# Two decode layers on one core: seven of the streamed tiles are fetched by three DMAs of 112, 8 and 8 partitions instead of one DMA of 128

## The chip, the cores and the metric

The kernel runs on one core of a Trainium2 chip. The metric is the device time of one execution in microseconds; lower is better. The time before is a median of three executions, and one more execution was profiled.

## The reference, cut to what matters

Two layers of attention against a cache, each followed by a dense layer with a gelu, are run twice over the same weights and caches, for one new position of eight sequences (B = 8, D = 1024, 32 query heads, 4 key and value heads of 128, 4096 cached positions, F = 3584), all in float32:

```python
def _A_ref(x, k_cache, v_cache, wq, wo):
    q = (x @ wq).reshape(B, Sq, Hq, Dh).transpose(0, 2, 1, 3)
    k = jnp.repeat(k_cache, rep, axis=1)
    v = jnp.repeat(v_cache, rep, axis=1)
    scores = jnp.einsum("bhqd,bhkd->bhqk", q, k) * (Dh ** -0.5)
    p = _softmax(scores, axis=-1)
    o = jnp.einsum("bhqk,bhkd->bhqd", p, v)
    return o.transpose(0, 2, 1, 3).reshape(B, Sq, Hq * Dh) @ wo

def _B_ref(x, w1, b1, w2, b2):
    h = _gelu(jnp.einsum("bsd,df->bsf", x, w1) + b1)
    return jnp.einsum("bsf,fd->bsd", h, w2) + b2

x = x + _A_ref(_layernorm(x), k_cache, v_cache, wq, wo)
x = x + _B_ref(_layernorm(x), w1, b1, w2, b2)
# and the same two lines once more
```

## The kernel before, in words

Eight rows of activations meet 134 MB of cache and some 63 MB of weights in each layer, so nearly all the work is to bring tiles from HBM into SBUF and to run each through TensorE once. Every tile is 128 partitions high. A tile is either "k = 4" (four columns of the arena, 4 x 4 KB = 16 KB in each partition, 2 MB in all) or "k = 2" (8 KB in each partition, 1 MB in all).

The order of all loads is written down ahead, in the list `stream`: the weights of the query projection (`q0`), then the caches of layer 0 in the order in which `scores` and `values` use them (`caches`), then `o0`, `i0`, `p0` (output projection, first and second dense matrix), `q1`, the caches of layer 1 in reverse order of sequences without what is still held from layer 0, and `o1`, `i1`, `p1`. The function `pump` takes the next entry of the list as soon as the `Arena` has room for it and issues its load on SyncE's queue (SP), one `dma_start` for a whole tile. `release` frees a tile after its last use and calls `pump` again, so SP's instructions stand in the order of the stream, each with its wait for the tile whose place it takes. The framework counts the DMAs of a queue on eight semaphores in turn, and a DMA that uses one again waits until the DMA eight places earlier has landed.

A tile has a key. For weights it is a name and a number (`("o0", 8)` is the ninth tile of the output projection of layer 0, `(("q1", 0), 2)` the third of the first half of the query projection of layer 1). For caches it is the layer and the piece: `(0, ("k", 2, 0, 0))` is layer 0, the keys of sequence 2, heads 0 and 1, first half of the positions; `(0, ("v", 4, 3, 0))` the values of sequence 4, head 3. Sizes follow from `pairs` and from the lists in the calls of `weights`: the cache tiles of sequences 0 to 5 in layer 0 and 0 to 4 in layer 1 and the tiles of `o1` have 2 MB, those of `o0`, `i0` and `q1` 1 MB.

`scores` (L295), `values` (L349), `expand` (L213) and `project` (L266) are the matmuls that read the tiles; each waits for its whole tile. The last tiles of the stream belong to `p1`, whose matmuls feed the last addition (L275) and the store of the output (L515).

Of the kernel before, what the change touches and what calls it, by code (L numbers as in the profile page):

```python
# [14 lines left out]
P = 128  # L15
# [21 lines left out]
N_TILE = 24  # L37
N_OWN = 2
EXTRA = 7
Q_AT = (0, 48, 72, 32)  # L40
QW = 88
DMA_SCRATCH = 1024
# [41 lines left out]
def decode_layers(ctx: ExitStack, tc: tile.TileContext, x, kc, vc, wq, wo, w1, b1, w2, b2, out):  # L84


    nc = tc.nc
# [84 lines left out]
    def pump():  # L172
        while stream:
            key, k, src, limit, pack = stream[0]
            arena.limit = min(limit, arena.cap)
            slot = arena.take(k, pack=pack)
            if slot is None:
                return
            stream.pop(0)
            if callable(src):  # L180
                src(slot.ap)
            else:
                nc.sync.dma_start(out=slot.ap[:, 0:src.shape[1]], in_=src)  # L183
            held[key] = slot

    def release(slot):
        slot.free()
        pump()
# [50 lines left out]
    def query_unit(u, row):  # L239
        src = turned(row, 2 * REP)  # L240
        for e in range(2):
            c = Q_AT[2 * u + e]
            nc.vector.tensor_copy(qz_v[:, c:c + REP, :], src[:, e * REP:(e + 1) * REP])
# [35 lines left out]
    def k_at(b, r):  # L279
        return b, r % HKV, r // HKV  # L280

    def v_at(b, r):
        return b, r // NH, r % NH

    def scores(at, kt, spare=False):
# [6 lines left out]
        ps = st["ps", half]  # L292
        c = b * QW + Q_AT[j] - REP * j
        for g in range(NG):
# [180 lines left out]
    kept = {("k", *k_at(B - 1, r)) for r in range(NR)} | {("v", *v_at(B - 1, r)) for r in range(NR)}  # L475
    kept |= {("k", *k_at(B - 2, NR - 1 - e)) for e in range(EXTRA)}
    first = [("k", B - 1, j, half) for half in range(NH) for j in range(2)]
# [17 lines left out]
    weights("i1", w1, [4, 4, 4, 2], [BIG] * 2)  # L495
    weights("p1", w2, [4] * 6 + [2, 1, 1], [BIG])
    pump()
    for layer in range(2):
        st["layer"] = layer
# [69 lines left out]
```

## Time and profile before

| | |
|---|---|
| median of three executions | 886.03 us (885.03 to 888.13) |
| the profiled execution | 886.38 us, of which 884.4 us from its first to its last instruction |
| mean granted TensorE clock | 0.809 |
| TensorE busy (matmuls) | 565.8 us, 64% |
| VectorE, ScalarE busy | 180.8 us, 47.2 us |
| moved by DMA | 371.15 MB, mean 420 GB/s |
| DMA's share of the chain that ended last | 85% |

The profiled execution is 0.35 us above the median, so its rows can be read against the median as they stand. "DMA share" in a row of the profile is the mean busy share of the core's sixteen DMA engines; "us to landing" is the median time from the issue of a DMA to the landing of its last byte.

### The profile page before, as it was taken

Reading aid. Unit: us, or ns where it says so; the run is one execution under the profiler, and the core shown is the slowest. Engines: PE = TensorE matmul, PEld = TensorE weight load, DVE = VectorE, ACT = ScalarE, POOL = GpSimd, SP = SyncE. Lnnn points to the kernel's source line nnn. Section 1 sums busy time; section 2 is a strip of 40 time slices with the busy share of each in tenths; the row PEclk is TensorE's granted clock in tenths of the full one; section 3 lists DMA queues with packets and bytes.
Section 4 is the critical chain, followed back from the end, with each engine's and each line's share of the span. In section 5 each row is a group of like instructions: output and inputs, shape, how many; then the busy total and the mean of one; then the engine's idle time right before and its main releaser. Section 6 shows DMA issues by size and latency. Waiting matters only on the chain.

```text
span 884.4 us, 9323 instructions
## 1 busy us (share of the span) xinstructions
PE 565.8 (64%) x4016; PEld 179.2 (20%) x4016; DVE 180.8 (20%) x586; ACT 47.2 (5%) x75; POOL 1.6 (0%) x11
## 2 busy tenths in 40 slices
PE   4565565565675767666656679956665575756766
PEld 1111121121111112222221122211121121222322
DVE  1002122221322223200200124422122222400110
ACT  2000000000000001001000100000000000000000
POOL 0000000000000000000000000000000000000000
PEclk9787788888868676867877979988888988876786
DMA  9999999999999999999999999999999999999996
GB/s 385 423 431 429 427 426 426 429 429 427 428 426 423 422 421 421 415 416 396 422 421 417 414 422 425 423 424 430 425 429 428 426 428 429 425 428 428 425 428 289
DMA packets 34888, 371.15 MB, mean 420 GB/s; under 512 B 4000, under 2 KB 4384, under 8 KB 4640
## 3 DMA queue, kind: packets, MB, share of 16 engines
q1 hardware_dynamic: 34704, 370.44, 99.5%
q8 instruction: 31, 0.51, 0.2%
q10 hardware_dynamic: 144, 0.13, 0.0%
q14 instruction: 9, 0.07, 0.0%
HBM read 370.42 MB, written 0.13 MB: 419 GB/s over the span
## 4 chain that ended last, share of the span: by engine, by line
DMA 85%; PE 11%; DVE 2%; issue 1%; ACT 1%; SPq 0%; ACTq 0%; DVEq 0%
DMA arena<-in_A_k_cache_dram 49%; DMA arena<-in_B_w_dram 17%; DMA arena<-in_A_wo_dram 8%; DMA arena<-in_A_wq_dram 7%; DMA arena<-in_A_v_cache_dram 4%; PE o_ps L349 2%; PE sps L295 2%; PE acc L213 2%; PE y L266 2%; DVE r_o L354 1%; PE sps L328 1%; PE sps L362 0%; SPq L183 0%; ACT arena L316 0%; PE s_ps L295 0%
## 5 line engine op out<-in xcount | busy, mean ns | idle before, releaser
L295 PE MATMUL sps<-arena,qz 128*32 128x512 f32 x992 | 169.3, 765 | 164.5 <-DMA arena<-in_A_k_cache_dram 162.7
L349 PE MATMUL o_ps<-arena 128*32 128x512 f32 x1024 | 166.1, 731 | 1.4 <-DMA arena<-in_A_v_cache_dram 1.4
L266 PE MATMUL y<-arena,oT 128*32 128x256 f32 x960 | 91.6, 532 | 54.1 <-DMA arena<-in_A_wo_dram 28.9
L213 PE MATMUL acc<-arena,xnT 128*32 128x512 f32 (+3 forms) x632 | 83.1, 625 | 47.2 <-DMA arena<-in_A_wq_dram 25.9
L295 PEld LDWEIGHTS sps<-arena,qz 128*32 128x32 f32 x992 | 24.7, 122 | 225.0 <-issue 139.4
L354 DVE SCALAR_TENSOR_TENSOR r_o<-o_ps,sel_t,r_o 128x128 f32<-128x128 f32 x192 | 67.4, 351 | 6.8
L266 PEld LDWEIGHTS y<-arena,oT 128*32 128x32 f32 x960 | 35.1, 141 | 109.5 <-DMA arena<-in_A_wo_dram 40.4
L349 PEld LDWEIGHTS o_ps<-arena 128*32 128x32 f32 x1024 | 35.0, 129 | 81.6 <-issue 79.2
L363 DVE TENSOR_TENSOR oT<-sps,rl 128x8 f32<-128x8 f32 x64 | 11.0, 173 | 179.7 <-PE sps L362 179.6
L316 ACT ACTIVATE arena<-arena,bias 128x1024 f32<-128x1024 f32 x16 | 18.4, 1148 | 520.9 <-DVE nb L313 520.9
L213 PEld LDWEIGHTS acc<-arena,xnT 128*32 128x32 f32 x632 | 23.6, 128 | 97.8 <-DMA arena<-in_A_wq_dram 42.7
L362 PEld LDWEIGHTS sps<-sel_h,r_o 128*128 128x128 f32 x128 | 23.5, 230 | 82.4 <-issue 53.1
L328 PE MATMUL sps<-ident,arena 128*128 128x128 f32 x128 | 22.7, 304 | 16.8 <-ACT arena L332 11.8
L298 DVE TENSOR_SCALAR_CACHE_REDUCE arena<-sps 128x512 f32<-128x512 f32 x31 | 21.4, 692 | 56.8 <-PE sps L295 56.8
L352 DVE TENSOR_SCALAR r_o<-o_ps,sel_t 128x128 f32<-128x128 f32 x64 | 22.4, 350 | 51.1 <-PE o_ps L349 51.1
L362 PE MATMUL sps<-sel_h,r_o 128*128 128x8 f32 x128 | 29.4, 302 | 4.4 <-DVE r_o L354 3.9
L275 DVE SCALAR_TENSOR_TENSOR x_row<-y,x_row 128x256 f32<-128x256 f32 x4 | 1.7, 425 | 122.4 <-PE y L266 122.4
L226 DVE TENSOR_SCALAR row<-acc,rs 128x512 f32<-128x512 f32 (+1 forms) x8 | 5.5, 685 | 87.1 <-PE acc L213 87.1
L328 PEld LDWEIGHTS sps<-ident,arena 128*128 128x128 f32 x128 | 14.6, 150 | 36.0 <-ACT arena L332 16.0
L334 DVE COPY arena<-sps 128x512 f32<-128x512 f32 x16 | 11.1, 692 | 44.4 <-PE sps L328 44.4
L336 PE MATMUL sps<-dl,ones 128*128 128x32 f32 x32 | 7.3, 312 | 12.5 <-DVE arena L334 12.5
L311 DVE TENSOR_REDUCE nb<-sps 128x32 f32<-128x128 f32 x16 | 4.6, 289 | 49.1 <-PE sps L309 49.1
(66 smaller groups left out, 128.0 us busy)
## 6 DMA issues: line engine op xcount, KB each, us to landing
arena<-in_A_k_cache_dram SPq DMA_DIRECT2D x44, 2048.0 KB, 39.1
arena<-in_A_v_cache_dram SPq DMA_DIRECT2D x44, 2048.0 KB, 39.1
arena<-in_A_v_cache_dram SPq DMA_DIRECT2D x32, 1024.0 KB, 19.8
arena<-in_B_w_dram SPq DMA_DIRECT2D x31, 1024.0 KB, 8.5
arena<-in_A_k_cache_dram SPq DMA_DIRECT2D x25, 1024.0 KB, 21.0
arena<-in_B_w_dram SPq DMA_DIRECT2D x12, 2048.0 KB, 36.7
arena<-in_A_wq_dram SPq DMA_DIRECT2D x8, 2048.0 KB, 23.0
arena<-in_A_wo_dram SPq DMA_DIRECT2D x16, 1024.0 KB, 8.1
```

Source lines behind the costliest of these rows:

```text
L213: nc.tensor.matmul(acc[32 * j:32 * j + 32, i0 * P:(i0 + ni) * P], xnT[:, kt * B:kt * B + 32], tv[:, s:s + 4 * ni - 3:4, :], start=(j not i ...
L266: nc.tensor.matmul(y[32 * j:32 * j + 32, 0:Q4], lhs[:, kt * B:kt * B + 32], slot.ap[:, c + j * Q4:c + (j + 1) * Q4], start=(kt == 0), stop ...
L295: nc.tensor.matmul(ps[32 * g:32 * g + 32, :], qz[:, c:c + 32], kt[:, g * CH:(g + 1) * CH], start=(j == 0), stop=(j == HKV - 1))
L298: nc.vector.tensor_scalar(st["row", b].ap[:, half * CH:(half + 1) * CH], ps, SCALE, None, op0=ALU.mult, op1=ALU.max, accum_out=st["mx", b] ...
L316: nc.scalar.activation(row, row, AF.Exp, bias=bias, scale=1.0, accum_out=ls)
L328: nc.tensor.transpose(pp[:, t * P:(t + 1) * P], row[:, c:c + P], ident)
L334: nc.vector.tensor_copy(dst, src)
L349: nc.tensor.matmul(o[32 * g:32 * g + 32, :], s[:, g], v[:, g * CH:(g + 1) * CH], start=(half == 0), stop=(half == NH - 1))
L352: nc.vector.tensor_scalar(r, o[:, 0:P], sel_t[:, 0:1], None, op0=ALU.mult)
L354: nc.vector.scalar_tensor_tensor(r, o[:, t * P:(t + 1) * P], sel_t[:, t:t + 1], r, op0=ALU.mult, op1=ALU.add)
L362: nc.tensor.matmul(po[:, 0:REP], st.pop(("r", b, j)), sel_h, start=True, stop=True)
L363: nc.vector.tensor_tensor(oT_v[:, j * REP:(j + 1) * REP, b], po[:, 0:REP], st["rl", b][:, j * REP:(j + 1) * REP], ALU.mult)
```

## The change: seven tiles are cut at partitions 112 and 120

Seven keys are listed. When `pump` comes to one of them it issues three DMAs instead of one, for partitions 0 to 111, 112 to 119 and 120 to 127, into the same place of the arena and from the same tensor, one after another on the same queue. All other tiles are loaded as before, the order of the stream is the same, and no byte more or less is moved. Four of the seven tiles have 2 MB (a key and a value tile of layer 0, a value tile of layer 1, a tile of `o1`), three have 1 MB (in `o0`, `i0` and `q1`).

```diff
 EXTRA = 7
+UNEVEN = {(0, ("k", 2, 0, 0)), (0, ("v", 4, 3, 0)), ("o0", 8), (("i0", 1), 0), (("q1", 0), 2), (1, ("v", 4, 2, 0)), ("o1", 6)}
+CUTS = (0, 112, 120, 128)
...
             if callable(src):
                 src(slot.ap)
             else:
-                nc.sync.dma_start(out=slot.ap[:, 0:src.shape[1]], in_=src)
+                cuts = CUTS if key in UNEVEN else (0, P)
+                for p0, p1 in zip(cuts, cuts[1:]):
+                    nc.sync.dma_start(out=slot.ap[p0:p1, 0:src.shape[1]], in_=src[p0:p1])
             held[key] = slot
```

## The prediction

> **What bounds the kernel now.** I read the page's head first, then the chain that ended last, the DMA issues, the waits, and then stretches of the span by engine.
>
> ```profile
> span 884.4 us, 9323 instructions
> ...
> DMA  9999999999999999999999999999999999999996
> ...
> q1 hardware_dynamic: 34704, 370.44, 99.5%
> q8 instruction: 31, 0.51, 0.2%
> q10 hardware_dynamic: 144, 0.13, 0.0%
> ...
> DMA 85%; PE 11%; DVE 2%; issue 1%; ACT 1%; SPq 0%; ACTq 0%; DVEq 0%
> ...
> L295 PE MATMUL sps<-arena,qz 128*32 128x512 f32 x992 | 169.3, 765 | 164.5 <-DMA arena<-in_A_k_cache_dram 162.7
> ```
>
> The sixteen DMA engines are busy in every slice, the last chain is DMA for 85%, and TensorE's largest idle time, 164.5 us ahead of the score matmuls, was ended by a landing nearly always. So whatever delays the DMA engine that finishes a tile last delays the kernel. The third part also tells how a DMA is cut. The one load on q10 (`x_row`, 128 partitions) has 144 packets, and 34704 is 241 times 144: each of the 241 DMAs on SP's queue is 128 packets, one for each partition, and 16 more, one for each engine.
>
> ```profile
> arena<-in_A_k_cache_dram SPq DMA_DIRECT2D x44, 2048.0 KB, 39.1
> ...
> arena<-in_B_w_dram SPq DMA_DIRECT2D x31, 1024.0 KB, 8.5
> ...
> arena<-in_A_wq_dram SPq DMA_DIRECT2D x16, 1024.0 KB, 8.2
> arena<-in_A_wo_dram SPq DMA_DIRECT2D x16, 1024.0 KB, 8.1
> ```
>
> ```profile
> 683.14 0.33 SPq L183 DMA_DIRECT2D arena<-in_A_v_cache_dram  x1
> 688.04 0.33 SPq L183 DMA_DIRECT2D arena<-in_A_k_cache_dram  x1
> ```
>
> In the cache stages one 2 MB tile is issued every 4.90 us (688.04 less 683.14) and lands 39.1 us later, so eight tiles are under way and 4.89 us is what one costs. Sixteen engines move 128 rows in that time, eight each: 0.61 us for a row of 16 KB, 0.31 us for one of 8 KB. The 1 MB tiles of `o0`, `i0`, `q1` land after 8.1 to 8.5 us, some three tiles (2.45 us each) under way.
>
> ```profile
> core 0: us, PE busy (x) PEld busy (x) DVE busy (x) ACT busy (x) POOL busy (x), PEclk, DMA share, GB/s
> ...
> 350.00:410.00 60.00, 42.19 (x374) 14.95 (x370) 9.04 (x30) 3.34 (x5) 0.00 (x0) 0.73 1.01 413
> 410.00:500.00 90.00, 57.22 (x530) 18.86 (x522) 7.22 (x24) 2.65 (x6) 0.00 (x0) 0.82 1.01 415
> ...
> 560.00:860.00 300.00, 190.39 (x1372) 64.27 (x1364) 67.97 (x224) 14.96 (x25) 0.00 (x0) 0.82 1.01 427
> ...
> 870.00:875.00 5.00, 3.64 (x32) 1.38 (x32) 0.00 (x0) 0.00 (x0) 0.00 (x0) 0.50 0.98 408
> 875.00:876.00 1.00, 0.36 (x4) 0.20 (x8) 0.00 (x0) 0.00 (x0) 0.00 (x0) 0.50 0.72 295
> 876.00:877.00 1.00, 1.00 (x16) 0.47 (x12) 0.00 (x0) 0.00 (x0) 0.00 (x0) 0.50 0.65 266
> 877.00:878.00 1.00, 1.00 (x16) 0.51 (x12) 0.00 (x0) 0.00 (x0) 0.00 (x0) 0.50 0.53 217
> 878.00:879.00 1.00, 1.00 (x17) 0.45 (x12) 0.00 (x0) 0.00 (x0) 0.00 (x0) 0.68 0.25 102
> 879.00:880.00 1.00, 1.00 (x28) 0.48 (x16) 0.00 (x0) 0.00 (x0) 0.00 (x0) 1.00 0.11 45
> ```
>
> The last six rows show what the change can be after. Nothing is left to issue, yet the engines do not stop together: the share falls from 0.98 to 0.11 over five microseconds. The idle parts add up to 0.10 + 0.28 + 0.35 + 0.47 + 0.75 + 0.89 = 2.84 us for each engine on average. Every engine was given the same rows, so some have lost time to others' work, such as the 31 instruction packets on q8. If all stopped together, the last byte would land 2.8 us earlier.
>
> **The change part by part.** *Fourteen more issues on SP.*
>
> ```profile
> L183 SPq DMA_DIRECT2D arena<-in_A_v_cache_dram x76: 327/328/438, 44.2 to 732.1; - x76
> ...
> SPq L183 <- DMA arena<-in_A_v_cache_dram: 234.5, 62, 4.9
> SPq L183 <- DMA arena<-in_A_k_cache_dram: 230.8, 60, 6.1
> ```
>
> Fourteen times 0.328 us is 4.6 us, in portions of 0.66 us. SP waits 465 us for landings in the cache stages, so this is covered there; in `o0`, `i0` and `q1` the tile queued behind is issued 0.66 us later and still has about 8 us until it lands. I take zero. Were that cover gone, the next tile would be late by at most 0.66 us each time, 4.6 us in all.
>
> *Three DMAs in place of one take three of the eight that may be under way.* Six tiles are then in flight for a while: 6 x 4.89 = 29 us of work in the cache stages, where a DMA starts with no delay as long as anything is queued. In the 1 MB stages three are under way now, so eight is no limit. Zero again. The matmuls that read the tile wait for three counts instead of one; what decides is the last of the three landings, priced below.
>
> *The rows are shared out differently.* 112 rows are seven for each of sixteen engines. Eight rows cannot occupy sixteen engines when a row is one packet; they occupy at most eight. If both short DMAs fall on the same eight, these carry nine rows of the tile and the other eight carry seven. The shift is one row each way: 4 x 0.61 + 3 x 0.31 = 3.4 us by the end, a gain if the eight are the early ones, a loss if they are the late ones. No row of this trace says which engines they are. [...]
>
> *Eight engines write eight neighbouring partitions.* This the trace before never shows: there a DMA always spans all 128 partitions, and an engine's eighth of a megabyte goes to eight partitions of its own, in 4.89 us. Bounds from that row: if the receiving side takes any eight rows at once, a short DMA costs each engine its one row, 0.61 us. If eight neighbouring partitions can take no more than eight partitions are seen to take, the short DMA lasts 8 x 0.61 = 4.89 us. I take the middle case, two groups of four: 4 x 0.61 = 2.44 us. The reason is that 16 engines run at the same rate, 427 GB/s, through keys, values and weights, so a fixed ceiling of 26.7 GB/s for each share of the partitions fits, while nothing says that the eight partitions of one engine are all neighbours. [...]
>
> The sum, for the eight engines: seven rows and two short DMAs, 7 x 0.61 + 2 x 2.44 = 9.2 us, instead of 4.9, so 4.3 us more for a 2 MB tile and 2.1 us for a 1 MB tile. 4 x 4.3 + 3 x 2.1 = 23.5 us. Two things take some back. Engines that are early may lose up to their lead: 2.8 us by the rows of the end. And the three 1 MB tiles stand between 350 and 500 us, where the rate is 413 to 415 GB/s rather than 427, 3% of 150 us or 4.6 us of gaps; I let half of it, 2.3 us, absorb delay. That leaves 18.4 us. What is late next is TensorE's wait for the landing (L295, L266), and through the count of eight every later issue. Against the profiled execution, 886.4 + 18.4 = 904.8; the median is 0.35 us lower, so 904.5 us.
>
> Seven-row shares no longer match the eighths of a 128-row DMA; that may cost nothing, or a row more for a tile, 3.4 us in all. I take nothing and leave the 3.4 us to the range.
>
> **The rivals.** *The shares are evened and nothing stands in the way.* The end then moves by up to 2.8 us, and since tiles are late by the same lag wherever the stream stalls on the last engine, the turn between the layers could give another 1.5 us, about half of that. The rows of the end speak for it; so does TensorE there:
>
> ```profile
> 875.64 4.68 PE L266 MATMUL y<-arena,oT 128*32 128x256 f32 x56 [1.27 <-DMA arena<-in_B_w_dram]
> ```
>
> TensorE starts this last run of 56 matmuls when a tile lands, 1.27 us after it was free, and can start 1.27 us sooner; beyond that it needs the tile before to land sooner too, which evened engines would do. Time 886.0 less 2.8 to 4.3, about 882.5. This is the rival on the other side, and it decides if a short DMA costs under about 0.75 us: the eight engines then take on 7 x 0.61 + 1.5 - 4.89 = 0.88 us for a 2 MB tile, 4.8 us over the four and the three halves, and five microseconds is the time over which the engines stop at the end. Against it: eight rows into one corner of SBUF have to go in unhindered.
>
> *It does nothing that counts.* The two short DMAs may fall on different engines, or the shift of 3.4 us may only make other engines the last ones. Time 885 to 888. For it: instruction packets take 0.2% of 16 x 884.4, some 28 us for all, 1.8 us for each engine if they are spread evenly, and then there is no half to relieve.
>
> *The wrong half is loaded.* Rows go to the engines that are late, without any crowding. The last landing moves by up to 3.4 us: 889.4. For it and against it the trace has nothing.
>
> *All eight rows go in line.* 7 x 0.61 + 2 x 4.89 = 14.1 us for a tile instead of 4.9, 9.2 us more; 4 x 9.2 + 3 x 4.6 = 50.6, time about 936. Against it: it needs eight neighbours to be one share.
>
> **How the numbers follow.** What a measurement of this kernel can tell from no change is about 0.3%, 2.7 us. Chances: crowding by fours 0.43 (of the bounds it has the only row of rate behind it, but no row shows the crowding); evened engines 0.24, of which 0.18 is over 2.7 us; nothing 0.17; the wrong half 0.09, of which 0.06 is over 2.7 us; in line 0.07. Slower: 0.43 + 0.06 + 0.07 = 0.56. Faster: 0.18. Within: 0.26. The range begins at 882, below which the evened case could go by another microsecond, and ends at 913: the 23.5 us without anything taken back and the 3.4 us of the seven-row shares. It leaves out the case in line and the edges of the first two, under 0.2. The likeliest case's own range is 896 to 913.
>
> **What the profile after would show.** If crowding is right: landings of the seven tiles later by about 4 us (2 MB) and 2 us (1 MB), a DMA share or rate that dips after each, and in the last rows a longer fall of the share, with about half of the engines far behind. q1 then has 241 x 144 packets plus the additional completions of fourteen DMAs. If the engines were evened, the fall from 0.98 to 0.11 shrinks to some two microseconds. If SP's issues mattered, its instructions at L183 would follow each other without a wait. The prediction is wrong if a short DMA costs its engines nothing beyond its one row; that is the step on which 18 of the microseconds hang.

## The result and the profile after

| | before | after |
|---|---|---|
| median (range) | 886.32 us (885.03 to 888.13) | 932.73 us (928.20 to 933.94) |
| ratio of the two | | 1.0515, 95% interval 1.0489 to 1.0541 |
| profiled execution | 886.38 us, span 884.4 | 933.94 us, span 931.9 |

Here both kernels have six executions, so the median of before is a little above that of the first three (886.03 us). The change costs 46.4 us. The sign was forecast; the size (18.4 us) was not, and the time lies 20 us above the range. From the page of the kernel after, its head, its DMA queues, its chain and the largest wait of TensorE:

```profile
span 931.9 us, 9352 instructions
...
DMA  9999999999999999999999999999999999999996
GB/s 389 425 429 427 290 428 427 428 427 428 428 260 426 421 421 421 400 364 351 403 421 327 388 423 425 422 427 378 345 430 426 427 429 428 426 390 300 427 425 275
...
q1 hardware_dynamic: 34816, 370.44, 99.4%
...
DMA 89%; PE 9%; DVE 1%; issue 1%; SPq 0%; ACT 0%; ACTq 0%; DVEq 0%
...
L299 PE MATMUL sps<-arena,qz 128*32 128x512 f32 x992 | 166.1, 750 | 194.1 <-DMA arena<-in_A_k_cache_dram 193.2
```

The row of rates in the page of before has no such holes:

```profile
GB/s 385 423 431 429 427 426 426 429 429 427 428 426 423 422 421 421 415 416 396 422 421 417 414 422 425 423 424 430 425 429 428 426 428 429 425 428 428 425 428 289
```

Two rows have to be read together here. The row "DMA" is 9 in every slice, as before, and q1 is busy for 99.4% of sixteen engines (99.5% before): the engines hardly ever stand still. Yet slices of 23 us that had 417 to 428 GB/s fall to 290, 260, 327, 345 and 300, and two that had 416 and 396 to 364 and 351, where the listed tiles are loaded. The same 370.44 MB went through engines that were as busy, only slower: of the packets of 16 KB that begin between 104 and 114 us, the median is busy for 1.21 us, against 0.61 us before. (What packets took in the other kernels is given below, with the experiments on the receiving side.) Matmuls take as long as before (166.1 us against 169.3 at the score line); their wait for landings grew from 162.7 to 193.2 us.

In stretches of two and four microseconds, the first listed tile (keys of sequence 2) looks like this. The last two columns are the DMA share, which reads above 1 in stretches as short as these, and the rate:

```profile
96.00:100.00 4.00, 1.38 (x16) 0.42 (x16) 0.81 (x3) 0.00 (x0) 0.00 (x0) 1.00 1.03 438
100.00:104.00 4.00, 2.71 (x26) 0.71 (x18) 2.11 (x8) 0.00 (x0) 0.00 (x0) 1.00 1.02 287
104.00:106.00 2.00, 0.00 (x0) 0.00 (x0) 0.52 (x2) 0.00 (x0) 0.00 (x0) 1.00 1.09 270
106.00:108.00 2.00, 0.00 (x0) 0.00 (x0) 0.00 (x0) 0.00 (x0) 0.00 (x0) 0.86 1.03 229
108.00:110.00 2.00, 0.00 (x0) 0.00 (x0) 0.00 (x0) 0.00 (x0) 0.00 (x0) 0.50 1.43 184
110.00:112.00 2.00, 0.00 (x0) 0.00 (x0) 0.00 (x0) 0.00 (x0) 0.00 (x0) 0.50 0.89 98
112.00:114.00 2.00, 0.00 (x0) 0.00 (x0) 0.00 (x0) 0.00 (x0) 0.00 (x0) 0.50 0.70 123
114.00:116.00 2.00, 0.31 (x4) 0.23 (x8) 0.00 (x0) 0.00 (x0) 0.00 (x0) 0.50 0.86 328
116.00:118.00 2.00, 2.00 (x10) 0.45 (x2) 0.00 (x0) 0.00 (x0) 0.00 (x0) 0.50 1.00 426
```

The rate is low for 16 us. Against 428 GB/s the bytes that did not come are 4 x 141 + 2 x (158 + 199 + 244 + 330 + 305 + 100) = 3236 kB (GB/s times us), which is 7.6 us of the full rate. There are two parts: some eight microseconds at 229 to 287, then four at about 100. TensorE's timeline has the wait that this makes, where the longest of its kind was 5.8 us before:

```profile
115.69 1.93 PE L299 MATMUL sps<-arena,qz 128*32 128x512 f32 x8 [12.97 <-DMA arena<-in_A_k_cache_dram]
```

The rows at the end answer to the last six of the prediction, shifted by the 47.5 us of the span:

```profile
917.50:922.50 5.00, 1.94 (x32) 0.94 (x32) 0.00 (x0) 0.00 (x0) 0.00 (x0) 1.00 0.93 384
922.50:923.50 1.00, 0.19 (x4) 0.19 (x8) 0.00 (x0) 0.00 (x0) 0.00 (x0) 0.86 0.53 217
923.50:924.50 1.00, 1.00 (x12) 0.40 (x10) 0.00 (x0) 0.00 (x0) 0.00 (x0) 0.50 0.33 135
924.50:925.50 1.00, 1.00 (x16) 0.45 (x12) 0.00 (x0) 0.00 (x0) 0.00 (x0) 0.50 0.18 74
925.50:926.50 1.00, 1.00 (x16) 0.54 (x12) 0.00 (x0) 0.00 (x0) 0.00 (x0) 0.50 0.12 49
926.50:927.50 1.00, 1.00 (x24) 0.48 (x16) 0.00 (x0) 0.00 (x0) 0.00 (x0) 0.94 0.12 49
```

The idle parts add up to 0.35 + 0.47 + 0.67 + 0.82 + 0.88 + 0.88 = 4.1 us, 1.2 us more than before. The fall is a little longer, not shrunk, but no half of the engines is far behind: that would hold the share near 0.5, where it stays for one microsecond only (0.53).

### The profile page after: what moved, and what is told of

Same layout as the page of the kernel before. It is cut to its first block, busy times and chain, and to the rows that moved or that the text cites. A ratio compares the mean times of both kernels' runs of the same rounds, so it can differ in the third digit from the quotient of the medians.

```text
span 931.9 us, 9352 instructions
## 1 busy us (share of the span) xinstructions
PE 565.3 (61%) x4016; PEld 177.9 (19%) x4016; DVE 180.3 (19%) x586; ACT 47.2 (5%) x75; POOL 1.6 (0%) x11
## 3 DMA queue, kind: packets, MB, share of 16 engines
q1 hardware_dynamic: 34816, 370.44, 99.4%
## 4 chain that ended last, share of the span: by engine, by line
DMA 89%; PE 9%; DVE 1%; issue 1%; SPq 0%; ACT 0%; ACTq 0%; DVEq 0%
DMA arena<-in_A_k_cache_dram 32%; DMA arena<-in_A_v_cache_dram 28%; DMA arena<-in_B_w_dram 13%; DMA arena<-in_A_wo_dram 9%; DMA arena<-in_A_wq_dram 7%; PE acc L217 2%; PE y L270 2%; PE sps L299 2%; PE o_ps L353 1%; SPq L187 0%; PE sps L332 0%; PE s_ps L299 0%; PE sps L240 0%; PE sps L313 0%; DVE arena L338 0%
## 5 line engine op out<-in xcount | busy, mean ns | idle before, releaser
L299 PE MATMUL sps<-arena,qz 128*32 128x512 f32 x992 | 166.1, 750 | 194.1 <-DMA arena<-in_A_k_cache_dram 193.2
L217 PE MATMUL acc<-arena,xnT 128*32 128x512 f32 (+3 forms) x632 | 86.9, 645 | 52.2 <-DMA arena<-in_A_wq_dram 28.5
L320 ACT ACTIVATE arena<-arena,bias 128x1024 f32<-128x1024 f32 x16 | 18.4, 1148 | 544.3 <-DVE nb L317 544.3
L332 PE MATMUL sps<-ident,arena 128*128 128x128 f32 x128 | 24.0, 317 | 16.5 <-ACT arena L336 11.8
L332 PEld LDWEIGHTS sps<-ident,arena 128*128 128x128 f32 x128 | 15.4, 157 | 35.9 <-ACT arena L336 16.1
L340 PE MATMUL sps<-dl,ones 128*128 128x32 f32 x32 | 7.4, 318 | 12.5 <-DVE arena L338 12.5
```

The lines of the kernel that those rows point to most:

```text
L217: nc.tensor.matmul(acc[32 * j:32 * j + 32, i0 * P:(i0 + ni) * P], xnT[:, kt * B:kt * B + 32], tv[:, s:s + 4 * ni - 3:4, :], start=(j not i ...
L299: nc.tensor.matmul(ps[32 * g:32 * g + 32, :], qz[:, c:c + 32], kt[:, g * CH:(g + 1) * CH], start=(j == 0), stop=(j == HKV - 1))
L320: nc.scalar.activation(row, row, AF.Exp, bias=bias, scale=1.0, accum_out=ls)
L332: nc.tensor.transpose(pp[:, t * P:(t + 1) * P], row[:, c:c + P], ident)
```

## The experiments

The theories after the result. **Short DMAs**: the two DMAs of eight rows cost far more than estimated. **Shares**: the 112-row DMA is dear, because its shares fall on partitions that other engines write at that moment. **Cut as such**: any further DMA costs, by its issue, its count of eight or its completions. In all the runs only the loop in `pump` or its constants change; the edit stands ahead of what was expected. A sum "over nothing" is against the run that loads none of the seven tiles; since they are four of 2 MB and three of 1 MB, it is divided by 5.5 to give a price for a 2 MB tile. The time before was 885.2 to 886.3 us in the different comparisons, so a sum across them carries about 1 us.

### Does a cut as such cost?

Three DMAs for each listed tile, but cut along the columns, so that each spans all 128 partitions:

```diff
-cuts = CUTS if key in UNEVEN else (0, P)
+n = src.shape[1]
+cuts = (0, n * 14 // 16, n * 15 // 16, n) if key in UNEVEN else (0, n)
 ...
-    nc.sync.dma_start(out=slot.ap[p0:p1, 0:src.shape[1]], in_=src[p0:p1])
+    nc.sync.dma_start(out=slot.ap[:, c0:c1], in_=src[:, c0:c1])
```

> The same seven tiles, three DMAs each of the same sizes (14/16, 1/16, 1/16), but cut by columns: each spans all 128 partitions. Crowding theory (engines that write into the same group of partitions at the same time take turns): nothing is crowded, 886 to 888 us. Count theory (every additional DMA costs a fixed time, by its issue, its count or its place among the eight under way; 46 us over 14 DMAs, 3.3 us each): 932 us. Half-the-engines theory (the loss comes from DMAs that occupy only eight of the sixteen engines): 886 to 888 us, all sixteen are used.

886.24 us, ratio 1.0008 (0.9998 to 1.0017). Fourteen more issues, three counts to wait for and three of the eight places of the queue are worth nothing, as the prediction had it. The 46 us hang on which partitions a DMA reaches.

### Other cuts of the partitions

```diff
-CUTS = (0, 112, 120, 128)
+CUTS = (0, 112, 128)
```

> The same seven tiles cut at partition 112 alone, 112 and 16 rows; both DMAs can occupy sixteen engines. Crowding: the 112-row DMA costs what it costs in the changed kernel (7 rows of about 1.1 us), the 16-row DMA has four engines to each group of partitions, 2.4 us; 7.6 + 2.4 - 4.9 = 5.1 us for a 2 MB tile, 28 us over 5.5 of them, 914 us. Count: seven additional DMAs instead of fourteen, 23 us, 909 us. Half the engines: no DMA uses only eight, 886 to 890 us.

```diff
-CUTS = (0, 112, 120, 128)
+CUTS = (0, 64, 128)
```

> The same seven tiles cut at partition 64, two DMAs of 64 rows, each on sixteen engines with four rows. Crowding: 64 partitions are half of the groups, two engines to a group, each half takes as long as the whole tile takes now, 4.9 us more for a 2 MB tile, 27 us in all, 913 us. Count: seven additional DMAs, 909 us. Half the engines: 886 to 890 us.

```diff
-CUTS = (0, 112, 120, 128)
+CUTS = (0, 32, 64, 96, 128)
```

> The same seven tiles cut into four DMAs of 32 rows, each on sixteen engines with two rows. It tells how the groups lie. [...] Crowding with groups of eight neighbours: four engines to a group, four DMAs of 4.9 us, 14.7 us more for a 2 MB tile, 81 us in all, 967 us. Count: 21 additional DMAs, 70 us, 956 us. Half the engines: 886 to 890 us.

Measured: cut at 112 alone 925.35 us (ratio 1.0446, 1.0424 to 1.0469); at 64 927.48 us (1.0479, 1.0457 to 1.0501); at 32, 64 and 96 928.94 us (1.0491, 1.0474 to 1.0509). All three cost about as much as the change, and with all sixteen engines in use: q1 has 34816, 34816 and 35040 packets, which is sixteen more than before for each further DMA. So engines left idle or loaded unevenly cannot be the main part. A count of DMAs does not fit either (909, 909 and 956 us were expected by it). Crowding fits in that the first two are alike, but its numbers (914 and 913) are 11 and 14 us too low; what they lack is taken up further on. For the third it gave 967 with groups of eight neighbours, 38 us too high. The stretches of the kernel cut at 64 show one simple rate:

```profile
106.00:108.00 2.00, 0.00 (x0) 0.00 (x0) 0.63 (x2) 0.00 (x0) 0.00 (x0) 0.72 1.09 238
108.00:110.00 2.00, 0.00 (x0) 0.00 (x0) 0.00 (x0) 0.00 (x0) 0.00 (x0) 0.50 1.00 205
110.00:112.00 2.00, 0.00 (x0) 0.00 (x0) 0.00 (x0) 0.00 (x0) 0.00 (x0) 0.50 0.99 217
112.00:114.00 2.00, 0.00 (x0) 0.00 (x0) 0.00 (x0) 0.00 (x0) 0.00 (x0) 0.50 1.01 221
```

With engines wholly busy (0.99 to 1.01) the rate is 205 to 221 GB/s, half of 428. Here each half of the partitions, 0 to 63 and then 64 to 127, took half of the rate. A quarter at a time (cut at 32, 64 and 96) costs hardly more than a half at a time: 43.1 us against 41.6, with stretches of 184 to 246 GB/s from 104 to 114 us. If groups of eight neighbours were the unit, 32 partitions would be four groups and go at a quarter, 967 us by the expectation. So 32 neighbours went no slower than 64 did. What follows rests on an estimate of the author's, worked out from these numbers and from those of the runs with 8, 16 and 64 rows below: a group is eight partitions that together take what one engine brings, four neighbours of one quarter and four of the quarter beside it (0 to 31 with 32 to 63, 64 to 95 with 96 to 127). Which four go with which no run shows.

### What each part of the tile costs by itself

Parts of the seven tiles are left out. Each kernel has another list of the rows loaded:

```diff
+parts = [] if key in UNEVEN else [(slice(0, P), slice(0, P))]
+for to, fro in parts:
+    nc.sync.dma_start(out=slot.ap[to, 0:n], in_=src[fro])
```

> The base for the three kernels beside it: the seven tiles are not loaded at all (the matmuls read what lies there). 4 tiles of 4.9 us and 3 of 2.45 us fall away, 27 us: 859 us by every theory.

```diff
+parts = [(slice(0, 112), slice(0, 112))] if key in UNEVEN else ...
```

> Of the seven tiles only the 112-row DMA is issued; 16 rows of each are left out. Crowding theory with seven-row shares that straddle the groups: 7.6 us for a 2 MB tile, 859 + 5.5 x 7.6 = 901 us. If the short DMAs alone make the loss and the 112 rows go at the usual pace, 4.3 us: 859 + 23.5 = 882.5 us.

```diff
+parts = [(slice(112, 120), slice(112, 120)), (slice(120, 128), slice(120, 128))] if key in UNEVEN else ...
```

> Of the seven tiles only the two 8-row DMAs are issued, for partitions 112 to 119 and 120 to 127; 112 rows are left out. Crowding by fours: 2 x 2.44 us for a 2 MB tile, 859 + 27 = 886 us. All eight in line: 2 x 4.9 us, 913 us. No crowding: 2 x 0.61 us at most, 859 to 866 us.

| loaded of the seven tiles | us | ratio, interval | over nothing | for a 2 MB tile |
|---|---|---|---|---|
| nothing | 863.81 | 0.9753 (0.9730 to 0.9776) | 0 | 0 |
| whole, one DMA (the kernel before, in this comparison) | 886.14 | 1 | 22.3 | 4.1 |
| rows 0 to 111 | 916.26 | 1.0333 (1.0310 to 1.0355) | 52.5 | 9.5 |
| rows 112 to 119 and 120 to 127 | 886.47 | 0.9993 (0.9975 to 1.0011) | 22.7 | 4.1 |
| all, 112 + 8 + 8 (the change) | 932.73 | 1.0515 (1.0489 to 1.0541) | 68.9 | 12.5 |

Two numbers expected were missed: nothing loaded came out 4.8 us above 859, and the 112 rows lie above both of theirs (901 by shares across groups, 882.5 by short DMAs alone). This is where the time went. The 112 rows cost more than twice a whole tile, though they are an eighth fewer: 52.5 - 22.3 = 30.2 of the 46.4 us are there before a short DMA is issued. The two short ones, 16 rows, cost by themselves what 128 rows cost, 22.7 us, close to the 26.8 of two times 2.44 us for 5.5 tiles; eight rows wholly in line would be 5.5 x 9.76 = 53.7, and a row for each engine 5.5 x 1.22 = 6.7. On top of the 112 rows they add 932.73 - 916.26 = 16.5. The stretches of the kernel with the 112 rows alone have the first part of the hole and lack the second (the stretch at 110 has 360, where the change has 98):

```profile
100.00:104.00 4.00, 2.69 (x26) 0.71 (x18) 2.13 (x8) 0.00 (x0) 0.00 (x0) 1.00 1.03 287
104.00:106.00 2.00, 0.00 (x0) 0.00 (x0) 0.49 (x2) 0.00 (x0) 0.00 (x0) 1.00 1.07 270
106.00:108.00 2.00, 0.00 (x0) 0.00 (x0) 0.00 (x0) 0.00 (x0) 0.00 (x0) 0.89 0.96 213
108.00:110.00 2.00, 0.00 (x0) 0.00 (x0) 0.00 (x0) 0.00 (x0) 0.00 (x0) 0.50 1.05 266
110.00:112.00 2.00, 0.00 (x0) 0.00 (x0) 0.00 (x0) 0.00 (x0) 0.00 (x0) 0.50 0.93 360
```

and with the short ones alone the second:

```profile
100.00:104.00 4.00, 2.41 (x22) 0.71 (x18) 2.38 (x9) 0.00 (x0) 0.00 (x0) 1.00 1.17 213
104.00:106.00 2.00, 0.00 (x0) 0.00 (x0) 0.24 (x1) 0.00 (x0) 0.00 (x0) 1.00 0.84 107
106.00:108.00 2.00, 0.56 (x4) 0.23 (x8) 0.00 (x0) 0.00 (x0) 0.00 (x0) 0.83 0.85 328
```

### Is it the receiving side?

The same source rows in DMAs of the same sizes, sent to neighbours or spread. First the two short DMAs, to every fourth partition:

```diff
+parts = [(slice(96, 128, 4), slice(112, 120)), (slice(97, 128, 4), slice(120, 128))] if key in UNEVEN else ...
```

> As the kernel beside it with the two 8-row DMAs alone, the same source rows, the same engines, the same sizes, but written to partitions 96, 100, ... 124 and 97, 101, ... 125, so that no two of a DMA are neighbours; 112 rows are left out and the others lie in other places. Crowding at the receiving side by groups of four neighbours: each row goes at its own pace, 859 to 866 us, some 20 us under the kernel with neighbours. If the loss lies at the source (neighbouring rows of HBM) or in the use of only eight engines: the same time as with neighbours, 886 us.

883.51 us, ratio 0.9987 (0.9967 to 1.0006): next to no gain over the 886.47 with neighbours, and far from the 859 to 866 that was expected of crowding. But the time alone says little. Among ScalarE's waits in its trace are now three rows that end with a landing, at the line of a copy into another tile:

```profile
ACT arena L337 <- DMA arena<-in_A_v_cache_dram: 48.4, 2, 29.1
ACT arena L337 <- DMA arena<-in_A_wo_dram: 46.9, 1, 46.9
ACT arena L337 <- DMA arena<-in_A_k_cache_dram: 34.7, 1, 34.7
```

The same line of before (L332 there) waits for TensorE alone. In the timeline the longest of them stands in the stage of `o1`, and the DMA engines run empty beside it (shares 0.09 and 0.22):

```profile
798.23 0.60 ACT L337 ACTIVATE arena<-sps 128x512 f32<-128x512 f32 x1 [46.90 <-DMA arena<-in_A_wo_dram]
```

```profile
795.00:800.00 5.00, 1.11 (x4) 0.71 (x4) 0.00 (x0) 0.60 (x1) 0.00 (x0) 0.50 0.09 36
800.00:805.00 5.00, 3.98 (x19) 1.19 (x19) 2.45 (x6) 0.00 (x0) 0.00 (x0) 0.58 0.22 49
```

The wait comes with the slice in steps of four, and it can hide what the spreading brings: the fifth and twelfth slices of the rate are 400 and 381 GB/s here, against 352 and 360 with neighbours. So a second pair leaves the tile of `o1` alone (it is loaded whole) and moves 64 rows of the other six in four DMAs of 16 (the 16-row DMAs of the cut at 112 had sixteen completions each, so a row for each engine), to neighbours or, for every DMA, to partitions four apart from 32 to 95, by the estimate 16 different groups:

```diff
+parts = [(slice(a, a + 16), slice(a, a + 16)) for a in range(32, 96, 16)] if key in UNEVEN else ...
```

> Six of the seven tiles (the one in o1 is loaded whole) are loaded only in part: 64 rows by four DMAs of 16 neighbouring rows each, to partitions 32 to 47, 48 to 63, 64 to 79, 80 to 95; the other 64 rows are left out. All sixteen engines take one row of each DMA. Base: 863.8 us of the kernel without the seven tiles and 4.9 us for the tile in o1, 868.7 us. Crowding with groups of four neighbours: four engines to a group, 4 x 2.44 = 9.8 us for a 2 MB tile, 4.5 tiles, 44 us: 913 us. No crowding: 4 x 0.61 us, 11 us: 880 us.

```diff
+parts = [(slice(32 + b, 96, 4), slice(32 + 16 * b, 48 + 16 * b)) for b in range(4)] if key in UNEVEN else ...
```

> [...] 64 rows are left out. Crowding on the receiving side: 4 x 0.61 = 2.4 us for a 2 MB tile, 868.7 + 11 = 880 us, 33 us under the kernel beside it. A loss at the source, or by the form of the DMA: 913 us, the same as beside it.

Neighbours 899.01 us (1.0150, 1.0130 to 1.0170), spread 878.58 us (0.9923, 0.9908 to 0.9939). The two have the same source rows, sizes and number of DMAs, and differ by 20.4 us. The fifth and twelfth slices of their rates say it again, 304 and 346 for neighbours:

```profile
GB/s 389 423 428 427 304 423 429 429 428 424 430 346 424 420 422 421 404 366 385 403 413 359 397 424 425 423 423 415 335 428 431 426 428 427 427 427 429 423 428 294
```

and 427 and 427 spread:

```profile
GB/s 388 423 428 428 427 427 428 426 430 426 429 427 420 424 421 421 411 406 418 410 420 371 403 424 424 423 424 431 426 426 430 428 427 428 426 426 428 426 427 304
```

What is slow is the side that receives. The spread run gave the 880 that was expected; neighbours cost less than the 913 of four in line, by 14 us. The spread run has ScalarE's waits too (up to 32.3 us, one of them in its fifth slice), but its rate does not fall beside them, so they can only make the 20.4 us too small.

The records of single packets say the same without a sum across runs. A packet of 16 KB takes 0.61 us in the kernel before (median, stretch 100:112), 1.25 us in the kernel cut at 64 (106:114), 1.24 us in that cut at 32, 64 and 96 (104:112), 2.31 us where the two short DMAs alone are loaded (102:106), 1.89 us with four DMAs of 16 neighbours (102:110) and 0.61 us with the same rows spread (92:112). By the estimate of groups, twice the 0.61 us is what two engines to a group would give, and 2.31 is nearly the four times of four engines to a group.

### One tile alone, early

Only the third tile of `q0`, before the caches, is cut:

```diff
-UNEVEN = {...}
-CUTS = (0, 112, 120, 128)
+UNEVEN = {(("q0", 0), 2)}
+CUTS = (0, 64, 128)
```

> One tile alone is cut at partition 64: the third tile of the query weights, about 15 us after the start, where all engines are still within 0.4 us of each other; no tile of the seven is cut. Crowding two deep, no more: 4.9 us, 891 us. If what the cut at 64 cost beyond that (41 us for 5.5 tiles, 7.5 us each) comes from engines being apart when they meet the cut: still 4.9 us here. If it belongs to the cut itself: 7.5 us, 893.5 us.

```diff
-UNEVEN = {...}
+UNEVEN = {(("q0", 0), 2)}
```

> The same early tile, cut as in the change at 112 and 120. From 46.4 us over 5.5 tiles: 8.4 us, 894.5 us, if the cost belongs to the cut; 5 to 6 us, 891.5 us, if part of it comes from the engines being apart.

891.73 us (1.0076, 1.0056 to 1.0097) and 892.84 us (1.0085, 1.0069 to 1.0101): 6.3 and 7.4 us for one 2 MB tile, both between the two numbers expected, so the times of this pair did not part the theories that it was meant to part. They do show that a delay of the first microseconds of the stream is still there at the end, some 870 us later. The change costs 46.4 / 5.5 = 8.4 us for a 2 MB tile: later delays are not absorbed either.

The traces say more than the times, since they have sixteen landings for each DMA of 128 partitions (3872 for the 242 DMAs of before), read here as one for each engine's part. In the trace of before, the sixteen engines land the second tile of `q0` within 0.34 us of each other, and the third comes 4.88 us after it (first landings 12.88 and 17.76 us). With the third cut at 64, the first landings are 12.81, 17.83 and 22.70 us: the two halves take 9.89 us, 5.0 more than the whole tile, two deep and no more. At the first of the seven tiles the engines are further apart: in the trace of before fourteen land the tile ahead of it within 0.5 us, the other two 1.7 and 1.9 us after the first. There the same cut costs 6.6 us: from the tile ahead to the tile behind it is 16.36 us (101.25 to 117.61) instead of 9.78 (101.47 to 111.25). So, as far as one trace of each kernel can show it, the part beyond two deep goes with engines being apart.

### Why 112 rows are dear: the same rows, moved by two partitions

That a DMA gives each engine neighbouring rows is again an estimate, which the next runs test. If it does, 64 rows from 32 on are sixteen fours in sixteen different groups, one for each engine. From 34 on each engine's four lies across two groups. Rows 0 to 63 reach eight groups only, in line with the 205 to 221 GB/s of the cut at 64. One DMA for each listed tile, the other 64 rows left out:

```diff
+parts = [(slice(32, 96), slice(32, 96))] if key in UNEVEN else ...
```

> Of the seven tiles only rows 32 to 95 are loaded, by one DMA (64 rows are left out). [...] Rows 32 to 95 are then 16 fours in 16 different groups, one for each engine: nothing crowds, and the tiles cost half of the 22.3 us that whole tiles cost over loading nothing, 863.8 + 11 = 875. Rival: a DMA of fewer than 128 rows is slow as such (its shares, its descriptors), at the rate of the cut at 64, which costs 63.7 us over loading nothing for two halves: one half 32, 895. Rival: only the partitions reached count (the sixteen fours are all reached): 875 too; the run with rows 34 to 97 parts these.

```diff
+parts = [(slice(34, 98), slice(34, 98))] if key in UNEVEN else ...
```

> Of the seven tiles only rows 34 to 97 are loaded, by one DMA (64 rows are left out). The same number of rows, engines, packets and groups of four as with rows 32 to 95, but every share of four rows now lies across two groups, as the shares of seven in the 112-row DMA do. If shares that lie across groups are what made the 112 rows dear: worked out with each group of eight partitions serving its writers at 0.61 us for a row, the DMA takes 3.7 us alone and 4.3 us within the stream instead of 2.44 for a 2 MB tile, 5.5 x 1.8 = 10 us more than rows 32 to 95, about 885. If lying across costs nothing: the same as rows 32 to 95, 875.

```diff
+parts = [(slice(0, 64), slice(0, 64))] if key in UNEVEN else ...
```

> Of the seven tiles only rows 0 to 63 are loaded, by one DMA (64 rows are left out). Theory of groups: 16 engines write into eight groups, two into each, at half rate: between 863.8 + 22 = 886 (half rate alone) and 895 (half of what the cut at 64 costs over loading nothing). Rival, that only rows count: 875, as rows 32 to 95.

And all rows, cut at 32 and 96:

```diff
+parts = [(slice(0, 32), slice(0, 32)), (slice(32, 96), slice(32, 96)), (slice(96, 128), slice(96, 128))] if key in UNEVEN else ...
```

> The change with its cuts at 32 and 96 in place of 112 and 120; the whole result is computed. Theory of groups: rows 32 to 95 go at full rate (11 us over loading nothing), each of the two 32-row DMAs at half rate, as in the cut at 32, 64 and 96, where four of them cost 65.1 us: two cost 32.6. Sum 863.8 + 11 + 32.6 = 907. Rival, that a cut costs by being a cut: 927 to 929, as with one cut at 64 and with three at 32, 64 and 96.

| rows | us | ratio, interval | over nothing | for a 2 MB tile | 2 MB tile, worked out by groups |
|---|---|---|---|---|---|
| 32 to 95 | 874.50 | 0.9877 (0.9847 to 0.9907) | 10.7 | 1.9 | 2.4 |
| 34 to 97 | 887.59 | 1.0017 (1.0003 to 1.0031) | 23.8 | 4.3 | 4.3 |
| 0 to 63 | 906.19 | 1.0226 (1.0174 to 1.0277) | 42.4 | 7.7 | 4.9 |
| 0 to 31, 32 to 95, 96 to 127 | 925.36 | 1.0438 (1.0403 to 1.0473) | 61.6 | 11.2 | 7.3 |

The last column is an estimate: every engine takes its neighbouring rows in order at 0.61 us each, a group that two engines write at once gives each of them half its pace (after the 1.25 us of the cut at 64), and whole tiles stand ahead and behind. Moving the 64 rows by two, in the source and in SBUF, costs 13.1 us; nothing else differs between those two kernels. The pair of sixteens has shown that it is the receiving side that counts; that a source two rows further on costs nothing here was not tested by itself. Rows 32 to 95 cost half of a whole tile to within half a microsecond (10.7 against 22.3 / 2), so a DMA of fewer than 128 rows is not slow as such. Their rates have no hole at all in the fifth and twelfth slices:

```profile
GB/s 384 423 432 427 428 428 424 428 429 427 431 423 424 423 420 421 414 401 420 421 421 407 403 422 424 425 421 431 425 430 427 428 426 429 429 427 426 427 426 301
```

from 34 on they read 400 and 376:

```profile
GB/s 385 426 430 426 400 429 428 428 427 427 430 376 421 423 421 422 406 365 380 420 423 381 406 424 423 422 427 418 390 427 428 428 428 427 426 428 367 424 429 294
```

Shares of seven rows, 0 to 6, 7 to 13 and so on, would lie across groups nearly everywhere, and so the same reason should hold for the 112 rows; this pair shows it at another size of share. By groups the 112 rows come out at 6.4 us for a 2 MB tile, against 9.5 measured over the seven tiles. For engines in step the trace of the early tile bears the 6.4 out: the 112 rows take 6.6 us there (first landings 12.90 and 19.54 us), where seven rows at 0.61 us would be 4.3. Rows 0 to 63 and the cut at 32 and 96 missed their numbers the same way, by 2.8 and 3.9 us for a tile: the first was expected at 886 to 895 and came to 906, the second at 907 and came to 925, no better than the other cuts. The stretches of rows 0 to 63 show what the estimate lacks:

```profile
102.00:104.00 2.00, 1.89 (x16) 0.35 (x16) 1.03 (x4) 0.00 (x0) 0.00 (x0) 0.98 1.20 229
104.00:106.00 2.00, 0.00 (x0) 0.00 (x0) 1.60 (x6) 0.00 (x0) 0.00 (x0) 1.00 0.92 188
106.00:108.00 2.00, 0.00 (x0) 0.00 (x0) 0.00 (x0) 0.00 (x0) 0.00 (x0) 1.00 0.89 197
108.00:110.00 2.00, 0.00 (x0) 0.00 (x0) 0.00 (x0) 0.00 (x0) 0.00 (x0) 0.73 0.96 246
```

One megabyte at half the rate takes 4.9 us, but the rate stays at half for about nine: nearly as much again of the tiles ahead and behind goes at half rate too. The landings fit engines that are out of step. Of the tile ahead, fourteen engines are done by 102.3 us, but the two late ones only at 104.8 and 105.8; the tile behind comes 6.7 us after the half tile (first landings 106.46 and 113.15) instead of 4.9. Where the engines were in step, nothing outlasted the cut: behind the early tile cut at 64 the next one came 4.91 us later (22.70 and 27.61), behind the listed tile with the same cut 6.48 us (111.13 and 117.61). Which engine waits for which is not shown by any of these rows; that late engines meet early ones in each other's groups is argued from them.

## Why the prediction was wrong in size

- **Fourteen issues, three of the eight places, three counts: nothing.** Right; cut by columns the kernel costs what it did (1.0008).
- **A short DMA uses eight engines.** Right: q1 has 34816 packets, 112 more than before, fourteen times eight completions; with sixteen it would be 224. Which eight they are no run shows. The sum put both short DMAs of a tile on the same eight, which no run shows directly either; the trace of the early tile fits it: of the tile behind, eight engines land at 28.4 to 28.9 us and the other eight at 29.7 to 30.1.
- **A short DMA is crowded, by fours.** Right: a packet took 2.31 us, where 2.44 was the estimate and 0.61 the lower bound, and 16 rows cost 22.7 us by themselves, where 26.8 was the estimate and 6.7 the bound. So it was not luck that the sign came out. The rival of evened engines needed under 0.75 us for each, 1.5 for the two; 4.1 was measured for a tile's two.
- **"Seven-row shares ... I take nothing and leave the 3.4 us to the range."** This is the step that failed. It counted rows for each engine (seven, 4.27 us) and asked only whether shares of tiles match in length. The 112 rows cost 9.5 us for a 2 MB tile, and over seven tiles 30.2 us more than whole tiles, two thirds of the loss. The prediction had priced crowding where eight engines write eight neighbours and did not ask where sixteen shares of seven begin. The same 64 rows moved by two partitions cost 13.1 us more, which the estimate puts down to engines that meet where their shares lie across groups. 6.4 to 6.6 us of the 9.5 are accounted for so; the rest goes with engines that reach the tile apart, and how they meet stays open.
- **What is taken back, 2.8 and 2.3 us.** Wrong. The 2.8 rested on a loss that falls on eight engines and leaves the early ones a lead to spend; the 112 rows slow all sixteen (in the early tile even the first landing comes after 6.6 us, where seven rows at 0.61 us are 4.3). The 2.3 rested on gaps between 350 and 500 us, and the slices there fell to 364 and 351. One tile at the start still costs 7.4 us at the end.
- **The sum, redone.** Forecast was 5.5 x (4.27 + 4.88 - 4.88) = 23.5 less 5.1. Measured: 52.5 for the 112 rows in place of 23.5, 16.5 for the short ones on top in place of 26.8, 22.3 for the whole tiles in place of 26.8. These three give back the whole loss because they are differences of the same runs; what they tell is which terms were off. The 112 rows were 29.0 us too low, the short ones 10.3 and the whole tiles 4.5 us too high, and 5.1 us were taken back in vain: 29.0 - 10.3 + 4.5 + 5.1 = 28.3, the 28 us between the forecast's 18.4 and the measured 46.4.
- **The rival nearest in time**, eight rows in line with 936, had the wrong reason: 16 rows would then cost 53.7 us by themselves, not 22.7, and the cut at 32, 64 and 96 would come to 967, not 929.

Whole tiles never showed any of this: in the trace of before a packet of 16 KB took 0.61 us (median; between 560 and 700 us 95 of 100 took 0.62 us or less), and the stretch from 560 to 860 us ran at 427 GB/s. Which rows a DMA hands to which engine no run shows directly; 64 rows from 32 on went without loss (1.9 us for a 2 MB tile), and 64 rows from 34 on did not (4.3).

## What to carry to other kernels

Leave streamed tiles at all 128 partitions, and cut them along the columns where they must be cut: that cost nothing here, and every cut of the partitions cost 39 us or more for seven tiles. Where fewer rows are loaded, ask for each engine's share which partitions it writes and who else writes there, not only how many rows it has; rows 32 to 95 went at full rate (428 and 423 GB/s in the fifth and twelfth slices) and rows 0 to 63 cost almost twice a whole tile (7.7 against 4.1 us). Here a DMA row of nines beside a rate that fell to 260 GB/s came from engines that were held up and did not lack work; they were held up where they write, which took the pair of neighbours and spread rows to show.

## What the runs showed of the hardware that was not expected

- Two partitions' shift of the same 64 rows is worth 13.1 us over seven tiles (874.5 to 887.6).
- The two short DMAs of 8 rows cost as much as the 128 rows of a tile (22.7 and 22.3 us), and 112 rows more than twice that (52.5).
- Rows 0 to 63 of the first listed tile, 1 MB, held the rate at 188 to 246 GB/s for some nine microseconds, where half rate explains 4.9, so the tiles ahead and behind went slower too; of the tile ahead two landings came late (104.8 and 105.8 us, the other fourteen by 102.3). With engines in step (within 0.34 us) a tile cut in halves cost 5.0 us more and the next tile nothing.
- A packet of 16 KB that took 0.61 us took 1.25 us in halves of 64 rows and 2.31 us in DMAs of eight neighbouring rows, and the engine counted as busy all the while.
- With slices in steps of four partitions ScalarE waited up to 46.9 us for loads into another tile. That the order drawn from such a slice is wider than the rows that it names is only argued.
